# Hash attention and a gated feed-forward on one core: a divisor placed earlier, two pools exchanged, half of the weight sums queued behind the first blocks

## The chip, the cores and the metric

The kernel runs on 1 core of one Trainium2 chip. The metric is the device time of one execution in microseconds (us). A measurement is the median of several executions; a profile is one further execution, with a trace of every engine: TensorE (PE, with its weight loads shown apart as PEld), VectorE (DVE), ScalarE (ACT), GpSimd (POOL) and SyncE (SP), whose work here is to start DMA transfers.

## What is computed

```python
# q, k, v: (4, 8, 768, 64); proj: (64, 6); w_in: (512, 2048); w_out: (2048, 512)
q_bucket = sum(((q @ proj) > 0) * 2**arange(6))      # the same for k_bucket
mask   = q_bucket[..., :, None] == k_bucket[..., None, :]
scores = where(mask, (q @ k.T) / sqrt(64), -1e9)
attn   = softmax(scores) @ v                          # per head
x      = attn.transpose(0, 2, 1, 3).reshape(3072, 512)
h      = x @ w_in
sp     = maximum(h, 0) + log1p(exp(-abs(h)))
out    = (h * erf(sp)) @ w_out                        # (3072, 512)
```

A query attends only to keys in the same hash bucket. The result of the attention, one row per token, goes through two matrix products with a smooth gate between them.

## The kernel before

**Attention.** The 32 heads are taken as 16 pairs. A pair `i` has four groups of scores (`score`, L554): two halves of the queries by two halves of the keys, three key blocks each. ACT takes the exponential of each block (`exponential`, L581), PE weighs the values with it (`weigh`, L639), and DVE adds the exponentials over the key blocks (`sum_keys`, L627, five steps for a pair). `divisor` (L680) lets PE add these sums over the partitions into a PSUM room, `keep_divisor` (L691, ACT) copies it to the tile `z`. The division then goes by small transfers on SP: `spread` (L720) writes `z` to DRAM, `gather` (L727) reads it back as 128x12, `invert` (L737, L740, DVE) takes the reciprocal, `ungather` (L745) and `widen` (L755, two transfers) spread it over the partitions, `normalise` (L766, DVE) multiplies, and `send` (L774) stores the pair's part of x. The last pair, 15, has its own path: its sums go in single steps, and its divisor to `send` are called from the feed-forward, as `late(0)` to `late(2)`.

**Weights.** Beside the attention, 32 pieces of the weights are fetched by POOL (`fetch_weights`, L460) and converted from 64-bit: `square_high` (L474) and `keep_normal` (L481) on ACT, `move_bits` (L488, L496), `mask_bits` (L510, L518) and `add_rest` (L528, L536) on DVE. `square_high` of piece n reuses the buffer that `mask_bits` of piece n-2 reads. `PACE` says after which exponential a piece may be fetched: after number PACE * n / 10 - 2.

**Feed-forward.** x is taken in 6 tiles of 512 tokens and 4 chunks of the hidden size, 24 blocks p. Both products save one of eight multiplications by Strassen's way: a block of the first product has seven products `P1` to `P7` (L1241), which share a few PSUM rooms. `read` (L1259, ACT) takes a room's first result into the tile `h`, `complete` (L1263, DVE) adds the second to it. A later product into the same room waits for that. Then come `lead`, `factor` and `saturate` on ACT (L1271, L1275, L1292), `multiply` and `gate` on DVE (L1281, L1296), sums of h (L1311), and the second product `M1` to `M7` (L1354). The sums that the method needs are made on DVE: of x by `presum_x` (L343) after `load_x` (L331), of w_in by `presum_weights` (L792, eight steps: four in the attention, four as `late(3)` to `late(6)`), of w_out by `presum_w` (L1326), kept by `keep_w` (L1329).

**What sets the order.** `arrange` is a list scheduler that runs when the kernel is built. It gets operations with an engine, an assumed cost, a rank, the operations each comes after, and lateness for signals; it emits them in the order in which they would start. Each engine then works through its own stream in this order, and waits at the first instruction whose semaphores aren't there. The attention (with the weights) is one such plan, the feed-forward with `late(k)` a second. The PE's order in the attention is written out by hand (`order`); the assumed costs move only what the other engines do between.

**Memory.** The attention's pools are closed before the feed-forward's are opened, which take the same memory from the start on. An instruction that first writes a tile of a new pool waits for the last uses of what lay there. The order of the attention's pools is loads of q, k and v (27 KB of a partition), hash bits, exponentials, then `xst` (tiles x, z, r). The feed-forward's: `hp` (h, 8 tiles of 4 KB), `sums`, `wtp` (sums of w_out), `work` (the gate's tiles, 32 KB), `outp`. The last pair keeps its exponentials in the tiles of the loads, which the last steps of `sum_keys` read.

Of the kernel before, what the change touches and what calls it, by code (L numbers as in the profile page):

```python
# [193 lines left out]
def kernel(  # L194
# [12 lines left out]
    B, H, S, D = v.shape  # L207
    NBIT = proj2.shape[1] // 2
    NPAIR = B * H // 2
# [3 lines left out]
    HS = S // 2  # L213
# [203 lines left out]
    def attention():  # L417
        NS = NPAIR * 4
        with (
# [10 lines left out]
            def big(name):  # L430
                return psum.tile([P, 2, 512], F32, name=name, tag="big", bufs=3)
# [9 lines left out]
            pairs = {}  # L441
# [205 lines left out]
            def home(i, what):  # L647

                if i < NPAIR - 1:
                    shape, bufs = {"x": (S, 3), "z": (HS, 1), "r": (S, 2)}[what]  # L650
                    return xst.tile([P, shape], F32, name=what, tag=what, bufs=bufs)
                rows = blocks[1][:, :, :].rearrange("p k t -> p (k t)")
                if what == "x":
                    return x_last, rows[:, 2 * S : 2 * S + HS]
                return rows[:, 0 : HS if what == "z" else S]
# [11 lines left out]
            def divisor(i):  # L667


                d = pairs[i]  # L670
                if i == NPAIR - 1:
                    z = bank("z_ps")[:, 0:HS]
                else:
                    room = pairs[i + 3]["bits"] if i + 3 < NPAIR else big("z_ps")
                    z = room[:, 1, 0:HS]
                d["z_ps"] = z
                for half in range(2):
                    for n in range(4):
                        ab, part = divmod(n, 2)
                        nc.tensor.matmul(  # L680
                            out=z[n * QR : (n + 1) * QR, half * HS // 2 : (half + 1) * HS // 2],
                            lhsT=ones[:, 0:QR],
                            rhs=d["sum"][:, half, ab, part * HS // 2 : (part + 1) * HS // 2],
                            start=True,
                            stop=True,
                        )
# [130 lines left out]
            def op(fn, args, engine, cost, rank, after=(), **more):  # L817
                name = (fn.__name__,) + args
                ops.append(Op(name, engine, cost, rank, lambda: fn(*args), after=after, **more))
# [77 lines left out]

            chain = []
            order = []
            PACE = 19  # L900
            for i in range(NPAIR):
                order += [("score", 4 * i + k) for k in range(4)]
                if i == 0:
                    order.append(("bits", 1))
                if i == NPAIR - 1:
                    order.append(("divisor", i - 1))
                order += [("weigh", 4 * i + k) for k in range(4)]
                if i + 2 < NPAIR:
                    order.append(("bits", i + 2))
                if 0 < i < NPAIR - 1:  # L910
                    order.append(("divisor", i - 1))
            slots = []
            for what, n in order:
                free = slots[-3] if len(slots) >= 3 else ()
                if what == "score":
                    i = n // 4
                    after = (("double_first",) if i == 1 else ("place_bits", i),)
                    for c in range(GC):
                        free = slots[-3] if len(slots) >= 3 else ()
                        pe(score, (n, c), 0.82 if n or c == 2 else 0.17, after + free)  # L920
                        slots.append((("exponential", n, c),))
                elif what == "bits":
                    pe(bits_of, (n,), 0.80 if n > 1 else 1.44, (("start_pair", n),) + free)
                    slots.append((("sign_of", n),) if n > 1 else (("place_first",),))
                elif what == "divisor":
                    if n + 3 < NPAIR:
                        free = ()
                        slots[-1] += (("keep_divisor", n),)
                    else:
                        slots.append((("keep_divisor", n),))  # L930
                    pe(divisor, (n,), 0.72, (("sum_keys", n, last_sum(n)),) + free)
                else:
                    h = n // 2
                    after = (("exponential", n, GC - 1),)
                    if n % 2 == 0:
                        after += (("leave", h - 2), ("leave_plain", (h - 2) // 2))
                    pe(weigh, (n,), 2.0, after)
# [5 lines left out]
            for n in range(NS):  # L943
                for c in range(GC):
                    after = (("score", n, c), ("weigh", n - 4)) + sums_after.get((n - 4, c), ())
# [8 lines left out]
            for i in range(NPAIR):  # L954
                for k, (what, blocks_) in enumerate(sum_steps(i)):
                    after = tuple(("exponential", 4 * i + b // GC, b % GC) for b in blocks_)
                    after += (("sum_keys", i, k - 1), ("sum_keys", i - 1, last_sum(i - 1)))
                    if k == 0:
                        after += (("divisor", i - 2),)
                    if i == NPAIR - 1 and k > 1:  # L960
                        after += (("divisor", i - 1),)
                    wide = what is None or what[2] > 1
                    rank = (3 if i == NPAIR - 1 and k > 2 else 1, 4 * i + 1 + k // 2, k)
                    op(sum_keys, (i, k), "DVE", 1.72 if wide else 0.92, rank, after)
            for i in range(NPAIR - 1):
                op(
                    keep_divisor,
                    (i,),
                    "ACT",
                    0.48,  # L970
                    (0, 4 * i + 6, -1),
                    (("divisor", i), ("spread", i - 1)),
                )
            for h in range(NH):
                i = h // 2
# [3 lines left out]
            for i in range(NPAIR):  # L979
# [52 lines left out]
                    (("ungather", i), ("normalise", i - 2)),  # L1032
                    late=6.5,
                )
                op(normalise, (i,), "DVE", 0.95, (0, n + 8, 4), (("widen", i), ("leave", 2 * i + 1)))
                op(send, (i,), "SP", 0.35, (0, n, 4), (("normalise", i),), late=2.2)
            for n in range(2):
                op(clean, (n,), "POOL", 1.4, (0, 4 * n), (("score", 4 * n + 3, 2),), late=0.3)
            for n in range(len(pieces)):
                op(  # L1040
                    fetch_weights,
                    (n,),
                    "SP" if n < 2 else "POOL",
                    1.0,
                    (0, n),
                    (("start_pair", 1), ("fetch_weights", n - 1), ("add_rest", n - 3), ("exponential", max(PACE * n // 10 - 2, 0), 1)),
                    late=7.0,
                )
                fetched = ("fetch_weights", n)
                op(square_high, (n,), "ACT", 0.68, (1, n, 0), (fetched, ("mask_bits", n - 2)))  # L1050
                op(keep_normal, (n,), "ACT", 0.7, (1, n, 1), (("square_high", n),))
                op(move_bits, (n,), "DVE", 1.05, (2, n, 0), (fetched, ("add_rest", n - 2)))
                op(mask_bits, (n,), "DVE", 1.1, (2, n, 1), (("move_bits", n), ("keep_normal", n)), late=1.5)
                op(add_rest, (n,), "DVE", 1.3, (2, n, 2), (("mask_bits", n),))
            for k in range(4):
                op(
                    presum_weights,
# [136 lines left out]
    def feed_forward(check, late):  # L1194
        again = late is None
        with (
            tc.tile_pool(name="hp", bufs=8) as hp,
            tc.tile_pool(name="sums", bufs=1) as sums,
            tc.tile_pool(name="wtp", bufs=2) as wtp,
            tc.tile_pool(name="work", bufs=1) as work,  # L1200
            tc.tile_pool(name="outp", bufs=1) as outp,
            tc.tile_pool(name="ps_f", bufs=1, space=PSUM) as ps_f,
            tc.tile_pool(name="ps_l", bufs=1, space=PSUM) as ps_l,
# [217 lines left out]
            def op(name, engine, cost, rank, fn, args, **more):  # L1421
                ops.append(Op(name, engine, cost, rank, lambda: fn(*args), **more))
# [132 lines left out]
            def second_ops(p):  # L1555
# [48 lines left out]
                if p < NC4 and not again:  # L1604
                    for k in range(4):
                        op(
                            ("presum_w", p, k),
                            "DVE",
                            0.69,
                            (2, p, k),  # L1610
                            presum_w,
                            (p, k),
                            after=(("presum_w", p, k - 1) if k else ("presum_w", p - 1, 3),),
                            take=("wt", p) if k == 0 else None,
                        )
                    op(
# [83 lines left out]
            if late:  # L1700
# [11 lines left out]
                        late=6.0,  # L1712
                    )
                for k in range(3, 7):
                    op(("late", k), "DVE", 1.2, (2, 1, -7 + k), late, (k,), after=(("late", k - 1),) if k > 3 else ())
                for each in ops:
                    if each.name in (("P5", 2), ("P6", 2), ("P7", 2), ("P3", 2)):
                        each.after += (("late", 6),)
# [107 lines left out]
```

## Time and profile before

| what | value |
|---|---|
| time, 3 runs | 917.02, 918.65, 919.42 us; median 918.65 |
| profiled execution | 916.7 us, its span 914.9 us |
| PE busy | 897.7 us, 98% of the span |
| DVE, ACT busy | 668.7 us (73%), 562.9 us (62%) |
| attention | from the start to about 315.5 us, some 19.17 us a pair |
| feed-forward | from 315.5 us; the last matmul ends at 908.3 us |

The profile gives for every group of instructions its line, engine, output and inputs, the count, the time that it was busy and the mean of one, and the idle time of the engine just before with what ended it ("<-"). The timeline has one row for each run of equal instructions: start, duration, engine, line, and in brackets how long the engine had been idle and who released it. Numbers are us from the start of the span. A matmul of the program shows as two records; a product P of the first kind is 8 records of about 0.216 us, 1.73 us in all.

### The profile page before, as it was taken

To read this page: it belongs to the slowest core of one execution; us is meant where nothing else is said; L and a number is where in the kernel's file an instruction comes from. 1 tells how busy PE (TensorE), PEld (TensorE's weight loads), DVE (VectorE), ACT (ScalarE), POOL (GpSimd) and SP (SyncE) were. 2 spreads that over 40 slices of the span, in tenths; PEclk is the share of its full clock that TensorE was granted. 3 is DMA by queue.
4 is the path that set the end of the run, shared out by engine and by line. 5 is a ranking of instruction groups with operands and counts; after the bars stand their busy time and mean duration, and the time that the engine had idled before them with its cause. 6 is when DMAs were issued, how large, how long until landed. Compare 5 with 4: busy or idle time off the path is not lost.

```text
span 914.9 us, 12791 instructions
## 1 busy us (share of the span) xinstructions
PE 897.7 (98%) x5016; PEld 673.0 (74%) x5016; DVE 668.7 (73%) x837; ACT 562.9 (62%) x808; POOL 58.2 (6%) x95
## 2 busy tenths in 40 slices
PE   9999999999999979999999999999999999999997
PEld 5455544545555558888888888888888888888886
DVE  5999997889989958996566656766676556655652
ACT  7788877778877538854655456555655555545520
POOL 1211211111110000000010001000100000000000
PEclk9999999999999989999999999999999999999999
DMA  9466555567553331021042114211321123101321
GB/s 227 130 166 166 154 175 146 151 189 188 140 171 99 100 122 64 2 80 60 22 104 81 35 47 104 81 35 47 81 104 35 35 58 92 34 31 52 69 69 49
DMA packets 65156, 86.82 MB, mean 95 GB/s; under 512 B 34364, under 2 KB 47772, under 8 KB 65088
## 3 DMA queue, kind: packets, MB, share of 16 engines
q1 hardware_dynamic: 56528, 63.81, 23.6%
q0 software_dynamic: 8112, 21.66, 8.5%
q8 instruction: 41, 0.67, 0.3%
q10 hardware_dynamic: 448, 0.46, 0.2%
q14 instruction: 27, 0.22, 0.1%
HBM read 64.67 MB, written 17.30 MB: 90 GB/s over the span
## 4 chain that ended last, share of the span: by engine, by line
PE 87%; DMA 5%; DVE 5%; ACT 1%; issue 1%; SPq 0%; POOL 0%; DVEq 0%; ACTq 0%; POOLq 0%
PE M L1354 32%; PE X L1241 28%; PE st L554 13%; PE av L639 9%; PE M L1241 2%; DMA r<-rd 2%; DMA rd<-zc 1%; PE bits L838 1%; DMA zd<-z 1%; DVE area L792 1%; DVE area L627 1%; PE bits L680 1%; DMA zc<-zd 1%; DVE x L766 1%; PE warm L800 0%
## 5 line engine op out<-in xcount | busy, mean ns | idle before, releaser
L1281 DVE SCALAR_TENSOR_TENSOR e<-w,e 128x1024 f32<-128x1024 f32 x144 | 173.8, 1220 | 10.3 <-ACT w L1275 5.9
L1241 PE MATMUL X<-area,w_in_sb 128*128 128x256 f32 x680 | 160.7, 379 | 0.0
L1275 ACT ACTIVATE w<-h,cq 128x1024 f32<-128x1024 f32 x144 | 155.5, 1136 | 0.0
L554 PE MATMUL st<-q,k 64*128 64x384 f32 x768 | 155.1, 483 | 0.0
L1263 DVE TENSOR_TENSOR h<-X,h 128x512 f32<-128x512 f32 x65 | 44.8, 689 | 145.0 <-PE X L1241 144.9
L1241 PEld LDWEIGHTS X<-area,w_in_sb 128*128 128x128 f32 x680 | 129.3, 190 | 17.5
L1354 PE MATMUL M<-w_out_sb,h 128*128 128x256 f32 x576 | 141.3, 379 | 0.0
L1241 PE MATMUL X<-area 128*128 128x256 f32 x520 | 123.0, 379 | 0.1
L1354 PEld LDWEIGHTS M<-w_out_sb,h 128*128 128x128 f32 x576 | 109.5, 190 | 14.8
L1259 ACT COPY h<-X 128x512 f32<-128x512 f32 x85 | 49.2, 579 | 110.7 <-PE X L1241 110.7
L1271 ACT ACTIVATE e<-h,cq 128x1024 f32<-128x1024 f32 x48 | 55.0, 1148 | 89.5 <-DVE h L1263 89.5
L1241 PEld LDWEIGHTS X<-area 128*128 128x128 f32 x520 | 98.8, 190 | 13.8 <-DVE h L1263 0.5
L1354 PE MATMUL M<-wt,S 128*128 128x256 f32 x384 | 95.1, 379 | 0.0
L554 PEld LDWEIGHTS st<-q,k 64*128 64x128 f32 x768 | 69.0, 187 | 29.9 <-issue 27.4
L627 DVE TENSOR_TENSOR area<-area 128x1536 f32<-128x1536 f32 (+1 forms) x46 | 79.3, 1724 | 3.4 <-ACT area L581 1.4
L1354 PEld LDWEIGHTS M<-wt,S 128*128 128x128 f32 x384 | 73.0, 190 | 9.9
L581 ACT ACTIVATE e_even<-st 128x768 f32<-128x768 f32 x96 | 70.3, 823 | 0.7 <-PE st L554 0.7
L581 ACT ACTIVATE area<-st 128x768 f32<-128x768 f32 x90 | 67.9, 813 | 0.0
L554 PE MATMUL st<-both 64*128 64x384 bf16 x384 | 63.7, 324 | 2.2 <-ACT z L691 1.7
L639 PE MATMUL av<-e_even,v 128*64 128x385 f32 x384 | 65.6, 490 | 0.0
L1296 DVE TENSOR_TENSOR h<-h,e 128x1024 f32<-128x1024 f32 x48 | 58.0, 1221 | 4.3 <-ACT e L1292 4.3
L639 PE MATMUL av<-area,v 128*64 128x384 f32 x360 | 60.6, 486 | 0.0
(129 smaller groups left out, 981.4 us busy)
## 6 DMA issues: line engine op xcount, KB each, us to landing
wt<-wt SPq DMA_DIRECT2D x24, 768.0 KB, 4.3
raw<-in_w_out_dram POOLq DMA_DIRECT2D x16, 512.0 KB, 4.6
raw<-in_w_in_dram POOLq DMA_DIRECT2D x14, 512.0 KB, 4.8
v<-in_v_dram SPq DMA_DIRECT2D x32, 192.0 KB, 4.7
q<-in_qkT_dram SPq DMA_DIRECT2D x30, 192.0 KB, 3.6
k<-in_qkT_dram SPq DMA_DIRECT2D x30, 192.0 KB, 4.2
r<-rd SPq DMA_DIRECT2D x30, 192.0 KB, 3.5
xs<-x SPq DMA_DIRECT2D x15, 384.0 KB, 2.5
```

The source lines that it names most:

```text
L554: nc.tensor.matmul(out=st[:, ab, 0:HS], lhsT=d["k" + src][rows, keys], rhs=d["q" + src][rows, cols], start=(part == 0), stop=(part == 1),)
L581: nc.scalar.activation(out=e[:, :, 0:HS], in_=st[:, :, 0:HS], func=AF.Exp, scale=scale)
L627: nc.vector.tensor_tensor(out=into, in0=one, in1=two, op=ALU.add)
L639: nc.tensor.matmul(out=d["av", half][rows, 0:w], lhsT=d["v"][:, g * GC + c, rows], rhs=e[:, ab, 0:w], start=(g == 0 and c == 0), stop=(g = ...
L1241: nc.tensor.matmul(out=d[where][:, u, :], lhsT=a[:, kc, f : f + P], rhs=b[:, kc, :], start=(first and u == 0 and kc == 0), stop=(last and ...
L1259: nc.scalar.copy(out=quarter(p, q), in_=st[p][where])
L1263: nc.vector.tensor_tensor(out=h, in0=st[p][where], in1=h, op=ALU.add)
L1271: nc.scalar.activation(out=s, in_=unit(p, v), func=AF.Sigmoid, bias=cq[:, n : n + 1])
L1275: nc.scalar.activation(out=q, in_=unit(p, v), func=AF.Sigmoid, scale=GATE_S[j][0], bias=cq[:, j : j + 1])
L1281: nc.vector.scalar_tensor_tensor(out=s, in0=st[p].pop(("q", v, j)), scalar=GATE_S[j][2], in1=s, op0=ALU.add, op1=ALU.mult,)
L1296: nc.vector.tensor_tensor(out=h, in0=h, in1=st[p].pop(("s", v)), op=ALU.mult)
L1354: nc.tensor.matmul(out=banks[name][:, sub, :], lhsT=a[:, u, sub * P : (sub + 1) * P], rhs=b[:, u, :], start=(c == 0 and k == 0), stop=(c = ...
```

## The change

- `divisor` of pair 14 is issued after the weighing of pair 14, right behind `divisor` of pair 13, and no longer between the scores and the weighing of pair 15. It uses the other half of the PSUM room of pair 13's divisor. `z` gets a second buffer, and `keep_divisor` waits for the spread of two pairs ago in place of one.
- `PACE` is 18 in place of 19, and the assumed cost of `sum_keys`, `normalise` and the conversion's steps on DVE is raised by some per cent. These are inputs to the scheduler.
- In the feed-forward, the pool `work` is opened first, before `hp`.
- `late(3)`, and with it the four steps of `presum_weights` in the feed-forward, and `presum_w` of block 1 get one more thing to come after: `complete` of block 0, quarter 1.

```diff
-                    shape, bufs = {"x": (S, 3), "z": (HS, 1), "r": (S, 2)}[what]
+                    shape, bufs = {"x": (S, 3), "z": (HS, 2), "r": (S, 2)}[what]
...
-                    room = pairs[i + 3]["bits"] if i + 3 < NPAIR else big("z_ps")
-                    z = room[:, 1, 0:HS]
+                    if i == NPAIR - 2:
+                        room = pairs[i - 1]["z_room"]
+                    else:
+                        room = pairs[i + 3]["bits"] if i + 3 < NPAIR else big("z_ps")
+                        d["z_room"] = room
+                    z = room[:, 0 if i == NPAIR - 2 else 1, 0:HS]
...
-            PACE = 19
+            PACE = 18
...
-                if i == NPAIR - 1:
-                    order.append(("divisor", i - 1))
                 order += [("weigh", 4 * i + k) for k in range(4)]
                 if i + 2 < NPAIR:
                     order.append(("bits", i + 2))
                 if 0 < i < NPAIR - 1:
                     order.append(("divisor", i - 1))
+                if i == NPAIR - 2:
+                    order.append(("divisor", i))
...
-                    if n + 3 < NPAIR:
+                    if n != NPAIR - 3:
...
-                    op(sum_keys, (i, k), "DVE", 1.72 if wide else 0.92, rank, after)
+                    op(sum_keys, (i, k), "DVE", 1.76 if wide else 0.93, rank, after)
...
-                    (("divisor", i), ("spread", i - 1)),
+                    (("divisor", i), ("spread", i - 2)),
...
-                op(normalise, (i,), "DVE", 0.95, (0, n + 8, 4), (("widen", i), ("leave", 2 * i + 1)))
+                op(normalise, (i,), "DVE", 1.02, (0, n + 8, 4), (("widen", i), ("leave", 2 * i + 1)))
...
-                op(move_bits, (n,), "DVE", 1.05, (2, n, 0), (fetched, ("add_rest", n - 2)))
-                op(mask_bits, (n,), "DVE", 1.1, (2, n, 1), (("move_bits", n), ("keep_normal", n)), late=1.5)
-                op(add_rest, (n,), "DVE", 1.3, (2, n, 2), (("mask_bits", n),))
+                op(move_bits, (n,), "DVE", 1.14, (2, n, 0), (fetched, ("add_rest", n - 2)))
+                op(mask_bits, (n,), "DVE", 1.15, (2, n, 1), (("move_bits", n), ("keep_normal", n)), late=1.5)
+                op(add_rest, (n,), "DVE", 1.4, (2, n, 2), (("mask_bits", n),))
...
+            tc.tile_pool(name="work", bufs=1) as work,
             tc.tile_pool(name="hp", bufs=8) as hp,
             tc.tile_pool(name="sums", bufs=1) as sums,
             tc.tile_pool(name="wtp", bufs=2) as wtp,
-            tc.tile_pool(name="work", bufs=1) as work,
...
-                            after=(("presum_w", p, k - 1) if k else ("presum_w", p - 1, 3),),
+                            after=(("presum_w", p, k - 1) if k else ("presum_w", p - 1, 3),) + ((("complete", 0, 1),) if p == 1 else ()),
...
-                    op(("late", k), "DVE", 1.2, (2, 1, -7 + k), late, (k,), after=(("late", k - 1),) if k > 3 else ())
+                    op(("late", k), "DVE", 1.2, (2, 1, -7 + k), late, (k,), after=(("late", k - 1) if k > 3 else ("complete", 0, 1),))
```

## The prediction, made before the changed kernel ran

> **What bounds the kernel now.** The page first: PE is busy 897.7 of 914.9 us, so the time is PE's work plus its gaps. Then PE's waits:
>
> ```profile
> PE M L1241 <- DVE h L1263: 5.3, 1, 5.3
> PE M L1241 <- ACT h L1259: 2.1, 1, 2.1
> PE st L554 <- ACT z L691: 1.7, 1, 1.7
> ```
>
> Columns: us in total, times, longest. With the small ones (1.0, 0.3, 0.2) and 6.6 us from the last matmul (908.3) to the end they make 17.2 = 914.9 - 897.7, so nothing else can be won as a gap. Where the two largest lie, the timeline shows:
>
> ```profile
> 319.52 0.96 DVE L627 TENSOR_TENSOR area<-area,v 128x768 f32<-128x768 f32 x1
> 320.71 0.59 ACT L1259 COPY h<-M 128x512 f32<-128x512 f32 x1 [4.59 <-DVE area L627]
> 321.35 3.72 PE L1241 MATMUL M<-area 128*128 128x256 f32 x16 [2.10 <-ACT h L1259]
> 324.10 1.02 DVE L766 SCALAR_TENSOR_TENSOR x<-x,ev,r 128x768 f32<-128x768 f32 x1 [3.61 <-DMA r<-rd]
> 327.56 1.22 DVE L792 TENSOR_TENSOR area<-w_in_sb 128x1024 f32<-128x1024 f32 x1
> 334.03 0.68 DVE L1263 TENSOR_TENSOR h<-M,h 128x512 f32<-128x512 f32 x1
> 334.77 7.99 PE L1241 MATMUL M<-area,w_in_sb 128*128 128x256 f32 x24 [5.26 <-DVE h L1263]
> ```
>
> The first `read` of the feed-forward waits for the last step of `sum_keys`: h lies over tiles that it reads. The second `complete` starts at 334.03, behind `presum_weights` and `presum_w` on DVE; its product had ended by 327.6. A third cost hides in the 24 matmuls after that: 334.77 to 342.60 is 7.83 us where 24 x 0.216 is 5.18. The windows (us, busy by engine, then granted clock, DMA share, GB/s) say why:
>
> ```profile
> 332.20:333.20 1.00, 0.00 (x0) 0.00 (x0) 1.00 (x2) 0.00 (x0) 0.00 (x0) 0.96 0.05 3
> 333.20:334.20 1.00, 0.00 (x0) 0.00 (x0) 0.97 (x3) 0.00 (x0) 0.00 (x0) 0.50 0.00 0
> 338.20:339.20 1.00, 1.00 (x4) 0.73 (x4) 0.00 (x0) 0.58 (x1) 0.00 (x0) 0.50 0.58 197
> 340.20:341.20 1.00, 1.00 (x6) 0.88 (x5) 0.00 (x0) 0.13 (x1) 0.00 (x0) 1.00 0.13 41
> ```
>
> The clock is halved from 333.2 to about 339.8. The stall thus costs 5.26 + 2.65. The gap in the attention:
>
> ```profile
> 201.52 0.67 ACT L474 ACTIVATE keep<-raw 128x512 f32<-128x512 f32 x1 [1.02 <-DVE top L510]
> 202.09 0.56 ACT L847 ACTIVATE sg<-bits,sgn 128x384 bf16<-128x384 f32 x1
> 202.56 0.47 ACT L691 COPY z<-bits 128x384 f32<-128x384 f32 x1
> 203.08 0.34 PE L554 MATMUL st<-both 64*128 64x384 bf16 x2 [1.68 <-ACT z L691]
> ```
>
> A `square_high` that needs DVE stands on ACT ahead of `sign_of` and `keep_divisor`, which free a PSUM room for the scores.
>
> [...] halved 3.8 us after the gap began at 329.4, no loss after the gap of 2.10. [...] Here the small ones take 1.4 to 5.4 us[...].
>
> **The change part by part**, on the time axis of before.
>
> *Pools.* In the changed build's order the first `read` no longer names `sum_keys` but the transfer of `send` of pair 14 (h now lies over x and r), with seven further semaphores behind it. `presum_w` names both sends. So what matters is when that send lands (before: issued at 325.14).
>
> *Divisor 14.* It moves from 306.84 to right behind divisor 13, which takes 296.26 to 297.05. PE's 0.79 and ACT's 0.47 move, nothing is added. It needs the last sum of pair 14, which ended at 296.90, so the wait costs 0 to 0.4; I take 0. On SP, spread and gather of 14 now stand between gather and ungather of 13, and on DVE its invert before the second sum of pair 15. The queues:
>
> ```profile
> 299.27 0.39 SPq L331 DMA_DIRECT2D area<-xs  x1
> 299.75 0.57 SPq L720 DMA_DIRECT2D zd<-z  x1
> 305.19 0.32 SPq L727 DMA_DIRECT2D zc<-zd  x1
> ```
>
> Spread 13 lands behind the 1 MB of `load_x`, so gather 13 stays at 305.19. `presum_x` now stands on DVE before the first sum of pair 15 and waits for that load: estimate 304.8, then 0.65 + 1.7, end 307.15. Spread 14 goes at 305.5, +2.0 (as 283.01 to 285.03) gather 14 at 307.6, +1.6 (as 250.36 to 251.99) 309.2, invert 0.45: DVE is free at 309.65. Then its list up to the end of `normalise` 14, each by the distance of starts in 307.78 to 319.52: two sums 1.67 + 0.93, one `presum_weights` 1.14, three `presum_x` 1.90, ev 0.07, two sums 0.98 + 0.88, `normalise` 13 0.93, sum 0.93, `normalise` 14 1.01, together 10.44: 320.1. The SP chain is just inside: ungather 14 after widen 13 at 310.65, +3.6, +4.2 = 318.5, needed at 319.1. Send at 320.2, +2.7 (median of xs<-x) 322.9; seven met semaphores at about 0.06, 323.4; `read` 0.59. PE resumes at 324.05, against 321.35: **+2.70**, an idle time of 4.8 in place of 2.10. With gathers and spreads of 3.4 each (269.93 to 273.28 is one) it is +5.9; with the SP and DMA steps 1 us better, +1.7.
>
> *Half of the sums later.* Behind the read, DVE has four `presum_w` (322.9 to 325.5), then the first `complete`; the second follows its product directly. PE doesn't wait there: **-5.26**, and the clock's 2.65 with it, if the new gap of 4.8 doesn't halve the clock itself. [...] So **-2.65**, or about 0. The four steps of `presum_weights` now lie at 332.5 to 337.4, where DVE idled for 6.0 (before 342.87). But `judge`'s small DVE steps (1.15) and three `multiply` stand ahead of a `complete` of block 1: DVE from 339 on 1.2 + wait to 340.9 + 1.15 + 2.3 + 0.65 gives 345, PE would ask at 344.3: **+0.8**, 0 to 1.5. After that PE has 14 us of products before it needs the first gate, which is then some 5 us early; the orders after it differ only in a few sums.
>
> *PACE and costs.* 32 pieces in both; each comes up to 1.5 score groups sooner, and none is left for pair 15, where one and its 3.7 us fall away from DVE. DVE needs 8.9 (five sums) + 1.7 + 3.7 x 2.22 = 18.8 of a pair's 19.17, so it may run some 0.9 late for a pair. In ACT's new order I went through all rows where `square_high` stands ahead of `keep_divisor`. The old place at 201.5 is clean. Two new ones are behind a `sign_of`: near 104.5, where DVE was 4 us ahead (cost 0.1), and near 180.7, where `mask_bits` ended at 181.7 in the trace of before: square 0.67 and z 0.47 after it, PE resumes at 183.05 where it wanted 182.1, +1.0. With 0.4 for small ones: 1.5 against 1.9, **-0.4**, from -1.9 to +3.
>
> *Sum.* +2.70 - 5.26 - 2.65 + 0.8 - 0.4 = **-4.8** us. The profiled execution, 916.7, becomes 911.9. It is 1.95 under the median of the runs, 918.65, to which I add the same difference: **913.8**.
>
> **Rivals.**
> - *The clock halves after all* in the gap before the first read. [...] Against: the gap of before was 5.26[...]. It hides the 0.8: -4.8 + 1.9 = -2.9, **915.7**.
> - *ACT's order costs more*: the places near 104.5, 120, 180.7 and 200 each stall PE by 1 us or so, since DVE has no slack left. For: 18.8 of 19.17, and waits for r and zc of up to 2.2. Against: DVE was early in the first pairs. -4.8 + 3.4 = -1.4, **917.2**.
> - *The send becomes the bound, slower.* Gather and spread of pair 14 take what spread 13 takes, 5.4, and 3.4; DVE stands behind invert, everything to the send lands 5.2 later, at 328.1. The gap of 10 surely halves the clock. -2.9 + 5.2 = +2.3, **920.9**. It decides from a landing at 325.8 on.
> - *All goes well*: the send lands at 321.9, no wait at judge, no stall at 180.7: -4.8 - 1.0 - 0.8 - 1.2 = -7.8, **910.9**.
> - *The change does nothing*: excluded, the built orders differ at each of these places.
>
> **How the numbers follow.** This kernel's runs spread by 0.26%, so about 0.3% (2.8 us) can be told from no change. Chances: forecast 0.43, halved clock 0.22, ACT's order 0.13, slower 0.12, all well 0.10. The forecast and all well lie under 915.9, and half of the halved clock's spread of 1 us or more: 0.64 faster. The rest of that, ACT's order, and a little of the slow case fall within 0.3%: 0.25; slower 0.11. The range takes in all well with its bound of 1 us and most of the slow side: 909.5 to 919.0.
>
> **What would show it.** In the profile after: PE's waits name `read` with 4 to 5.5 us and no `complete` with 5; the send of pair 14 lands near 323; the last z of the attention stands near 298; no halved clock around 333; a wait for z of about 1 us near 182 and none near 203. I am wrong if `read` waits past 326, if the attention's waits exceed 3 us, or if PE has a gap past 345 that I don't have.

## The result, and the profile after

| | before | after |
|---|---|---|
| time, median | 918.25 us (917.02 to 919.42, 4 runs) | 909.79 us (907.90 to 910.26, 4 runs) |
| profiled execution | 916.7 us, span 914.9 us | 910.26 us, span 908.2 us |
| PE busy | 897.7 us | 897.4 us |
| first product of the feed-forward | 315.53 us | 313.43 us |
| first matmul of the second product | 364.20 us | 358.23 us |

The changed kernel takes 0.9904 of the time before, with a 95% interval of 0.9884 to 0.9924. It is 8.5 us faster; 4.8 us were forecast, and the time lies just inside the range. PE is busy for as long as before; its gaps have changed. PE's three longest waits in the profile after (us in total, times, longest):

```profile
PE M L1245 <- ACT h L1263: 2.9, 1, 2.9
PE warm L804 <- DVE ones L250: 1.0, 1, 1.0
PE M L1245 <- DVE h L1267: 0.7, 1, 0.7
```

Lines from L676 on have moved by 4. The wait for a second `complete` (5.3) has become one of 0.7 at another place, and the attention's wait for `z` isn't there. The timeline where the feed-forward begins:

```profile
315.49 1.01 DVE L770 SCALAR_TENSOR_TENSOR x<-x,ev,r 128x768 f32<-128x768 f32 x1
...
318.84 0.69 DVE L1330 TENSOR_TENSOR wt<-w_out_sb 128x512 f32<-128x512 f32 x1 [0.48 <-DMA xs<-x]
319.45 0.59 ACT L1263 COPY h<-M 128x512 f32<-128x512 f32 x1 [5.43 <-DMA xs<-x]
320.09 6.63 PE L1245 MATMUL M<-area 128*128 128x256 f32 x16 [2.94 <-ACT h L1263]
...
329.54 0.69 DVE L1267 TENSOR_TENSOR h<-M,h 128x512 f32<-128x512 f32 x1 [7.48 <-PE M L1245]
331.00 5.34 PE L1245 MATMUL M<-area,w_in_sb 128*128 128x256 f32 x24
```

`normalise` of pair 14 runs at 315.49, 2.06 us after the first product; before it ran at 324.10, 8.57 after it. The transfer of its send has landed by 318.84, where `presum_w` on DVE was waiting for it; `read` follows at 319.45, PE after an idle time of 2.94. The second `complete` is on time, and DVE idles ahead of it. But the 16 matmuls at 320.09 take 6.63 us, where the same 16 took 3.72 before. The windows (us, busy by engine, then granted clock, DMA share, GB/s):

```profile
318.20:319.20 1.00, 0.00 (x0) 0.00 (x0) 0.52 (x2) 0.00 (x0) 0.00 (x0) 0.99 0.14 52
319.20:320.20 1.00, 0.11 (x1) 0.11 (x1) 0.97 (x3) 0.59 (x1) 0.00 (x0) 0.50 0.00 0
325.20:326.20 1.00, 1.00 (x4) 0.80 (x4) 0.00 (x0) 0.00 (x0) 0.00 (x0) 0.59 0.00 0
```

The clock is halved in this execution too, from 319.2 to 326.0, 2.0 us after PE went idle at 317.15. The place in the attention that the prediction feared:

```profile
177.56 0.69 DVE L510 SCALAR_TENSOR_TENSOR top<-top,keep 128x512 int32<-128x512 int32 x1
...
181.30 0.66 ACT L474 ACTIVATE keep<-raw 128x512 f32<-128x512 f32 x1
...
181.86 0.48 ACT L695 COPY z<-bits 128x384 f32<-128x384 f32 x1
```

A `square_high` does stand ahead of `z`, but the step of `mask_bits` that reads its buffer (`keep`, L510) had ended at 178.25, 3.0 us before it: PE doesn't wait.

### The profile page after: what moved, and what is told of

It reads as the page before. It is cut to its first block, busy times and chain, and to the rows that moved or that the text cites. A ratio compares the mean times of both kernels' runs of the same rounds, so it can differ in the third digit from the quotient of the medians.

```text
span 908.2 us, 12781 instructions
## 1 busy us (share of the span) xinstructions
PE 897.4 (99%) x5016; PEld 673.2 (74%) x5016; DVE 669.5 (74%) x837; ACT 563.3 (62%) x808; POOL 58.3 (6%) x95
## 4 chain that ended last, share of the span: by engine, by line
PE 96%; DVE 2%; DMA 1%; issue 0%; ACT 0%; SPq 0%; ACTq 0%; DVEq 0%
PE M L1358 32%; PE X L1245 29%; PE st L554 16%; PE av L639 13%; PE M L1245 3%; PE bits L842 1%; PE bits L684 1%; DMA zd<-z 1%; PE warm L804 0%; DVE area L627 0%; PE bits L374 0%; DMA xs<-x 0%; PE z_ps L684 0%; DMA zc<-zd 0%; DVE x L770 0%
```

## The experiments

They were run in four groups, each beside runs of the kernel before on its own chip; "ratio" is against those, with its 95% interval. Gaps of PE in us are from the one profiled execution of each: the waits for `z` in the attention, the one at the first `read`, and those for a `complete` (0.66 or 0.7 is the one behind `judge`, in block 1). "Halved" is for how many us of this execution the clock was halved, up to the last matmul. Times of different groups are compared by ratio. The groups are: the four kernels after with one part put back; after once more, the later sums alone, the gap filled and h placed early; the other three parts alone and h placed early with the weight sums put back; the last two rows.

| kernel | median, us | ratio to before | z | read | complete | halved |
|---|---|---|---|---|---|---|
| before | 918.25 | 1 | 1.7 | 2.10 | 5.26 | 6.8 |
| after | 909.79 | 0.9904 (0.9884 to 0.9924) | 0 | 2.94 | 0.66 | 6.8 |
| after, once more | 910.27 | 0.9908 (0.9887 to 0.9929) | 0 | 2.94 | 0.66 | 3.4 |
| after, pools put back | 907.53 | 0.9922 (0.9903 to 0.9941) | 0 | 2.04 | 0.66 | 0 |
| after, weight sums put back | 909.41 | 0.9938 (0.9919 to 0.9956) | 0 | 3.40 | 0.33 | 0 |
| after, divisor put back | 915.27 | 0.9993 (0.9984 to 1.0003) | 0 | 7.36 | 0.7 | 6.8 |
| after, PACE and costs put back | 912.92 | 0.9973 (0.9958 to 0.9987) | 1.5 | 3.91 | 0.66 | 3.4 |
| before, later sums alone | 912.34 | 0.9931 (0.9909 to 0.9954) | 2.1 | 2.18 | 0.66 | 3.4 |
| before, sooner divisor alone | 914.39 | 0.9964 (0.9953 to 0.9975) | 2.8 | 3.41 | 0 | 3.4 + 3.4 |
| before, PACE and costs alone | 913.67 | 0.9966 (0.9953 to 0.9978) | 0 | 0 | 5.33 | 6.8 |
| before, pools alone | 919.62 | 1.0019 (1.0008 to 1.0029) | 3.8 | 9.03 | 0 | 3.4 + 10.2 |
| after, gap filled on PE | 908.84 | 0.9904 (0.9886 to 0.9922) | 0 | 0.28 | 0.66 | 0 |
| after, h placed early | 905.71 | 0.9867 (0.9847 to 0.9886) | 0 | 0 | 0.66 | 0 |
| the same, weight sums put back | 910.46 | 0.9926 (0.9908 to 0.9943) | 0.2 | 0 | 2.94 | 3.4 |
| after, only the costs put back | 914.64 | 0.9967 (0.9952 to 0.9982) | 2.9 | 3.0 | 0.7 | 3.4 + 3.4 |
| after, only PACE put back | 916.61 | 0.9981 (0.9961 to 1.0001) | 6.6 | 3.5 | 0.7 | 10.2 + 3.4 |

### Each part put back, from the kernel after

The pools:

```diff
-            tc.tile_pool(name="work", bufs=1) as work,
             tc.tile_pool(name="hp", bufs=8) as hp,
             tc.tile_pool(name="sums", bufs=1) as sums,
             tc.tile_pool(name="wtp", bufs=2) as wtp,
+            tc.tile_pool(name="work", bufs=1) as work,
```

> The kernel after, with only the order of the feed-forward's pools put back (hp first, work fourth). Theory: each wait is where the trace of after shows it, and the pools set only what the first read waits for: no longer the transfer of the send of pair 14 (319.45 in after), but the last step of sum_keys (ends at 318.36). PE's first gap shrinks from 2.94 to about 2.1 us, the rest stays: about 908.9 us, or 907 to 908 where the shorter gap halves the clock for a shorter time. Then this part of the change costs some 0.9 us by itself. Rival: the pools are what keeps something else from waiting (the sums of w_out, the gate's first tiles): a new wait appears and it is slower than after, 911 or more.

The gap at the read shrinks to 2.04 us, as the theory has it, and its profile shows no halved clock. The ratio can't be told from that of after, so the 0.9 us stand on the profile alone. No new wait of PE of more than 0.2 us appears in its profile.

The weight sums:

```diff
-after=(("presum_w", p, k - 1) if k else ("presum_w", p - 1, 3),) + ((("complete", 0, 1),) if p == 1 else ()),
+after=(("presum_w", p, k - 1) if k else ("presum_w", p - 1, 3),),
...
-after=(("late", k - 1) if k > 3 else ("complete", 0, 1),))
+after=(("late", k - 1),) if k > 3 else ())
```

> The kernel after, with only the queue of the weight sums put back (late(3) and presum_w of block 1 free to stand ahead of the second complete). Theory of the prediction: the later sums are what took the stall of 5.26 us and its halved clock (2.65) away, so both come back, 909.8 + 5.3 + 2.6 = 917.7 us. Rival: the stall before was made by DVE being late behind normalise of pair 14, which the sooner divisor has moved from 324.10 to 315.49. DVE's list from 318.84 is then 4 x 0.66 + 4 x 1.22 + 0.68 + 2 x 0.66 = 9.5 us, so the second complete starts at 328.3; its product ends at about 329.3 in after with its halved clock, so there is no stall (909.8 us), or one of about 2 us where the clock isn't halved, 909.5 to 912 us in all.

The stall doesn't come back. PE's waits in its profile:

```profile
PE M L1245 <- ACT h L1263: 3.4, 1, 3.4
...
PE M L1245 <- DVE h L1267: 0.3, 1, 0.3
```

The second `complete` started at 328.19, where the rival's sum gave 328.3, and PE waited 0.33 us for it, without a halved clock. In this profile the later sums are worth next to nothing once the divisor is sooner; the prediction gave them the whole 5.26. The ratio alone doesn't show that: 0.9938 is some 3 us above that of after, in intervals that barely overlap. But beside the kernel with the pools put back, of the same group, it is 1.9 us slower by the medians, and the waits of the two profiles account for 1.7 of that (3.40 and 0.33 against 2.04).

The divisor of pair 14, with one buffer of `z` (the diff of the change backwards, its first, second, fourth and fifth piece and the line with `spread`):

> The kernel after, with only the divisor of pair 14 put back between the scores and the weighing of pair 15 (with one buffer of z and keep_divisor behind the spread of the pair before). Theory: with the pools of after the first read then waits for a send of pair 14 that follows normalise 14 at about 322 to 323; it lands at about 326, the gap grows from 2.94 to about 10 us and halves the clock as now: 909.8 + 7 = about 917 us. So the pools and the divisor belong together. Rival: the send isn't what the read waits for by much, and the gap is some 4 to 5 us: 911 to 912 us. For the attention: if its wait for z near 203 is back (1.7 us), it was the divisor's part of the change (second z, later spread) that removed it; if not, PACE and the costs.

The theory holds in kind: the `read` waits for the send, which was issued at 321.02 and had landed by 323.32. The gap is 7.36 us, in place of the 10 expected, with a halved clock behind it, and all but nothing of the gain is left. The attention has no wait for `z`, so it isn't the second `z` that emptied it.

PACE and the costs (19, and the old numbers):

> The kernel after, with PACE 19 and the old assumed costs. Theory: PACE and the costs are what emptied the attention of waits; ACT's order there is again that of before but for the end, so the wait for z near 203 comes back (1.9 us), and one piece of the weights with its 3.7 us on DVE stands in pair 15 again, so that normalise 14 and its send come up to 3.7 us later: 909.8 + 1.9 + 0 to 3.7 = 911.7 to 915.4 us. Rival: the second z buffer and the later spread emptied the attention, and PACE is worth nothing there: 909.8 to 910.5 us.

The median is within the theory's range: a wait for `z` of 1.5 us is back, and the gap at the read is 3.91 in place of 2.94.

### Each part alone, on the kernel before

The later sums alone:

> The kernel before, with the later weight sums alone (late(3) and presum_w of block 1 behind complete of block 0, quarter 1). Theory from the runs so far: the stall of 5.26 us comes from two things together, a late normalise of pair 14 (to 325.12) and the weight sums between it and the second complete; either part of the change removes it alone. Then DVE goes from 325.12 through four sums of w_out (2.6) and the first complete (0.7) to the second at 328.4, in time for the product at 329.4: no stall, 5.3 us won and its halved clock, the gap of 2.10 and the attention's 1.9 stay: some 6 to 8 us below before. Rival: only the sooner divisor removes it, and the time is that of before less 0 to 2 us.

No stall: `normalise` 14 ran at 326.11, the first and second `complete` in one go at 329.58, and PE went on at 331.17 without a wait. The ratio, 0.9931, is 6.3 us (4.2 to 8.4). So here the sums are worth what the prediction gave them. The profile has one thing more, a halved clock in the attention, from 185.43 to 188.85, after a wait of only 2.11 us:

```profile
184.19 0.34 PE L554 MATMUL st<-both 64*128 64x384 bf16 x2 [2.11 <-ACT z L691]
```

The sooner divisor alone:

> The kernel before, with the sooner divisor of pair 14 alone (second z, keep_divisor behind the spread two pairs ago). Theory: it removes most of the stall at the second complete by itself, since DVE no longer stands at normalise 14 until 325.12: with the last sum at 320.9 as in the kernel with PACE put back, its list of 9.5 us ends at 330.4 and PE asks at about 329.5, a stall of 1.6 us in place of 5.26 and mostly no halved clock; the gap at the read is 2 to 2.6 us and the attention's wait for z stays: some 4 to 6 us below before. Rival: without the later sums the stall stays at 5 us: the time of before.

The stall of 5.26 goes here as well, in this kernel without the later sums:

```profile
PE M L1245 <- ACT h L1263: 3.4, 1, 3.4
PE st L554 <- ACT z L695: 2.8, 1, 2.8
```

```profile
318.50 3.72 PE L1245 MATMUL M<-area,w_in_sb 128*128 128x256 f32 x16
...
331.76 1.99 PE L1245 MATMUL M<-area,w_in_sb 128*128 128x256 f32 x8
...
333.86 0.69 DVE L1267 TENSOR_TENSOR h<-M,h 128x512 f32<-128x512 f32 x1
```

But only half of that is the divisor's. The second `complete` starts 15.36 us after the first product, where it was 18.50 before: 3.1 sooner. And PE comes to the fifth product 13.26 us after the first, where it was 10.26 (315.53 to 325.79): 3.0 later, for the gap at the read is 3.41 in place of 2.10, with a halved clock behind it. The ratio is 3.3 us, less than expected, as that gap, a wait for `z` of 2.8 and two halved clocks (the other one behind that wait) stand against it.

PACE and the costs alone:

> The kernel before, with PACE 18 and the new costs alone. Theory: it takes away the attention's wait for z near 203 (1.9 us) and shifts all that follows by as much; the stall at the second complete stays at about 5 us, as it hangs on the transfers behind the divisor, and so does its halved clock; the gap at the read is 2.1 us or up to 1 us less, as DVE has one piece less in pair 15: 2 to 3 us below before. Rival: the piece that pair 15 no longer has moves normalise 14 and the stall too: 4 us or more below before.

```profile
PE M L1241 <- DVE h L1263: 5.3, 1, 5.3
```

The stall stays to the tenth, as the theory said; the wait for `z` is gone, and so is all of the 2.10 at the read (up to 1 was expected): without the last piece of the weights DVE ends the last `sum_keys` at 317.0, 3.0 us after the first product, where it was 5.0 before. By the ratio 3.1 us, by the medians 4.1.

The pools alone:

> The kernel before, with the other order of the feed-forward's pools alone. Theory: the first read waits for the send of pair 14, whose normalise ends at 325.12; with 2.7 us to landing and 0.6 for the waits the read goes at 328.4, PE's first gap is 9.8 us, and the stall at the second complete shrinks to 0 to 1.9 us since PE comes there later: 9.8 to 11.7 us of gaps in place of 7.4, 2.4 to 4.3 us slower than before. Rival: the send isn't late enough to matter behind the last sum, the time is that of before.

```profile
PE M L1241 <- ACT h L1259: 9.0, 1, 9.0
PE st L554 <- ACT z L691: 3.8, 2, 2.9
```

Slower by 0.19%, 1.7 us, where 2.4 to 4.3 were expected: the send was issued at 328.57 and had landed by 330.88, PE waits 9.03 us at the read for it, and the stall at the second `complete` is hidden behind that. By itself this part of the change loses.

### The clock, and a better place for h

The kernel after once more, unchanged, and one whose gap PE fills with work on nothing. The latter's edit, ahead of the third product:

```diff
+                st["calls"] = st.get("calls", 0) + 1
+                if st["calls"] == 3 and not again:
+                    fill = bank("fill")
+                    for n in range(12):
+                        nc.tensor.matmul(out=fill[0:D, 0:P], lhsT=ones, rhs=ones[:, 0:1].broadcast_to([P, P]), start=True, stop=True)
```

> The kernel after, unchanged, on the same chip as the next three, to compare with them; and a look at whether another execution halves the clock in the same place. Theory: [...] some executions halve it after the gap of some 3 us and others don't, and the times spread by the 2.9 us that it costs: 906 to 910 us. Rival: it is halved in each execution, and the spread is something else.

> The kernel after, with 12 matmuls of 128 columns on ones, into a PSUM bank that nothing else uses at that time, queued on PE just ahead of the product that waits for the first read; they fill some 2.6 of its gap of 2.9 us. Theory: [...] the clock is never halved here, and 2.9 us are won in those executions where after has it: its mean falls by 1 to 2.9 us and its spread is smaller. Rival: the halved clock has another cause than PE's idling (the DMA traffic or the load of the other engines at that time): it is still there, and the time is that of after.

The second profile of after has the same gap of 2.94 us, and the clock is halved for 3.4 us rather than 6.8. In the ten timed runs of after the mean clock is 0.995 to 0.998, and 0.998 in the three fastest, 907.84 to 908.74. With the gap filled the clock isn't halved in the profile. First the row of the fill, then two windows:

```profile
317.71 2.88 PE L1226 MATMUL fill<-ones 128*64 128x128 f32 x24
```

```profile
318.20:319.20 1.00, 1.00 (x11) 1.00 (x10) 0.93 (x1) 0.00 (x0) 0.00 (x0) 1.00 0.91 356
320.20:321.20 1.00, 0.72 (x6) 0.45 (x5) 0.97 (x3) 0.59 (x1) 0.00 (x0) 1.00 0.00 0
```

PE idles 0.28 us at this place in place of 2.94, and all its six runs have a mean clock of 0.998 or 0.999, so the rival falls: here the halved clock goes with PE's idling. The ratio, 0.9904 against 0.9908 of the same group, doesn't show the gain; the medians differ by 1.4 us, which is inside the intervals.

Then h where nothing late lies: in the attention `xst` is opened first, in the feed-forward `hp` last.

```diff
+            tc.tile_pool(name="xst", bufs=1) as xst,
             tc.tile_pool(name="load", bufs=3) as load,
             tc.tile_pool(name="bitp", bufs=1) as bitp,
             tc.tile_pool(name="ep", bufs=1) as ep,
-            tc.tile_pool(name="xst", bufs=1) as xst,
...
-            tc.tile_pool(name="work", bufs=1) as work,
-            tc.tile_pool(name="hp", bufs=8) as hp,
             tc.tile_pool(name="sums", bufs=1) as sums,
-            tc.tile_pool(name="wtp", bufs=2) as wtp,
             tc.tile_pool(name="outp", bufs=1) as outp,
+            tc.tile_pool(name="wtp", bufs=2) as wtp,
+            tc.tile_pool(name="work", bufs=1) as work,
+            tc.tile_pool(name="hp", bufs=8) as hp,
```

> The kernel after, with its pools in another order: in the attention x, z and r (xst) first; in the feed-forward h last, so that h lies over the exponentials and the buffers of the weights' conversion, whose last reader is a step of sum_keys that ends at about 307.8. The first read then waits for nothing but its product. Theory: the gap of 2.94 goes, with it the halved clock, and nothing stands behind it, since the second product into that room has its read done by then and the first complete, at about 321.0 behind four sums of w_out, isn't needed before the second block: -2.9 and up to -2.9, 904 to 906 us beside 907 to 910 of after. Rival: the wait was covering another, the complete of quarter 3 or the divisor of pair 15 behind the last step of sum_keys: PE waits 1 to 3 us a little later, and 1 us or less is won.

```profile
PE warm L804 <- DVE ones L250: 1.0, 1, 1.0
PE M L1245 <- DVE h L1267: 0.7, 1, 0.7
```

The gap is gone and no other took its place. This is the fastest of all: 0.9867 of before, and 4.6 us below after by the medians of the same group. The same with the weight sums put back:

> The kernel with h placed early (c_h_early), with the queue of the weight sums put back to that of before. Theory: in the kernel after the later sums were worth only some 0.3 us because PE's wait at the first read (3.4 us with the sums put back) gave DVE the time to get through the list ahead of the second complete. Without that wait DVE needs, from 318.36, 4 x 0.66 + 4 x 1.2 + 0.68 + 2 x 0.66 = 9.4 us, the second complete ends at 328.5, and PE asks for it at about 324.9: a stall of some 3.6 us, in some executions with a halved clock: 905.7 + 3.6 + 0 to 2.9 = 909 to 912 us. Rival: the later sums are worth little anywhere: 906 us.

```profile
PE M L1245 <- DVE h L1267: 2.9, 1, 2.9
```

A stall of 2.94 us at the second `complete`, with a halved clock. So the later sums, worth 0.3 us in the profile with the sums put back into the kernel after, are worth some 5 once nothing holds PE back at the read (ratios 0.9926 and 0.9867).

### PACE or the costs

> The kernel after, with the old assumed costs, but PACE 18. Theory: a piece that is fetched sooner is also converted sooner on DVE, so mask_bits is done before the square_high that waits for it, whatever the exact order on ACT; and none is left for pair 15. PACE is all of it: no wait for z in the attention, a gap of about 2.9 us at the read, 908 to 910 us. Rival: the costs hold the order in which ACT's z comes ahead of a square_high: a wait for z of 1 to 2 us is back, 911 us.

> The kernel after, with PACE 19, but the new assumed costs. Theory (PACE is all of it): a wait for z of 1 to 2 us in the attention, and a gap of about 3.9 us at the read, as in the run with both put back: 912 to 913.5 us. Rival: the costs do it: no wait for z, 909 to 911 us.

The theory falls. PACE 18 with the old costs has a wait for `z` of 2.9 us, PACE 19 with the new costs one of 6.6; neither can be told from the kernel with both put back (0.9973). Either one alone gives an order on ACT in which a `square_high` waits for DVE ahead of `z`. In the last kernel:

```profile
199.55 0.17 DVE L741 TENSOR_SCALAR zc<-zc 128x12 f32<-128x12 f32 x1 [4.99 <-DMA zc<-zd]
199.91 5.35 DVE L627 TENSOR_TENSOR area<-area 128x1536 f32<-128x1536 f32 x3
206.42 0.69 DVE L510 SCALAR_TENSOR_TENSOR top<-top,keep 128x512 int32<-128x512 int32 x1
207.15 0.67 ACT L474 ACTIVATE keep<-raw 128x512 f32<-128x512 f32 x1 [6.34 <-DVE top L510]
207.72 0.46 ACT L695 COPY z<-bits 128x384 f32<-128x384 f32 x1
208.23 0.51 PE L554 MATMUL st<-both 64*128 64x384 bf16 x2 [6.59 <-ACT z L695]
```

`invert` stood 4.99 us on DVE for a `gather`; three sums and the mask came that much later, `square_high` waited for the mask, `z` for ACT, PE for `z`. What such a place costs depends on when a small transfer lands. That is argued, not tried; it fits the spread of these two kernels' runs (910.07 to 918.98, and 911.56 to 920.12) and the different waits for `z` in the kernels that share before's PACE and costs, 1.5 to 3.8 us. In the nine profiles of kernels with PACE 18 and the new costs, PE has no wait for `z` in eight and one of 0.2 us in the ninth; in the seven others it has 1.5 to 6.6.

## Why the prediction was right in direction and short in size

The terms of the sum, forecast and as the two profiled executions have them:

| term | forecast | profiles |
|---|---|---|
| gap at the first read | +2.70 | +0.84 |
| second `complete` | -5.26 | -5.26 |
| halved clock | -2.65 | +0.26 |
| behind judge | +0.8 | +0.66 |
| attention | -0.4 | -2.1 |
| last stores land sooner | none | -0.7 |
| sum | -4.8 | -6.3 |

The profiled executions differ by 6.4 us, their spans by 6.7, so some 0.4 us of the spans are in no term. The medians differ by 8.46: the profile of before was 1.5 us below its median, that of after 0.5 above. Four steps failed.

- **"To which I add the same difference."** Of the 4.0 us between the forecast 913.8 and 909.79, 1.6 lie between the profiled execution that was forecast, 911.9, and 910.26. The other 2.4 are this term: the prediction put the median of after 1.95 above its profile, because it was so before, and gave no reason. It was 0.5 below. The profile of after is the slowest of its four runs, with the lowest mean clock (0.995; the others 0.996 to 0.998), so the halved clock is likely a part of it. Why the profile of before was faster than the four runs beside it stays open.
- **The attention's term, -0.4.** It counted a new wait of about 1.0 us near 180.7, from the end of a `mask_bits`, 181.7, in the trace of before. But PACE 18 also moves the pieces on DVE. The `square_high` that stands there after is the 22nd and waits for a step of the 20th `mask_bits`, which ended at 178.25 (181.7 is the end of this step of the 19th). The order on ACT was read rightly there, the time of its partner was not moved along. The attention lost its old waits (1.7 for `z`, 0.2 for an exponential) and got none: -2.1. That PACE and the costs do this, and only together, is shown by the runs with one put back.
- **"Gather 13 stays at 305.19", and "DVE is free at 309.65".** Set on the axis of before (+2.10), `gather` 13 went at 303.48, the load of x had landed by 303.4 (estimated 304.8) and the second `invert` ended at 308.27, 1.4 us early. From there the working held: DVE's list to the end of `normalise` 14 took 10.33 us (forecast 10.44), the send 2.3 (2.7), the semaphores and other waits ahead of `read` 0.6 (0.5). So the idle time was 2.94 in place of 4.8, and the term +0.84 in place of +2.70.
- **"So -2.65, or about 0."** That a gap of 4.8 us mostly spares the clock was the author's estimate: the trace of before had a halved clock behind a gap of 5.26 us, none behind one of 2.10, and no gap between. In the profile after the clock was halved behind 2.94, and the term is +0.26 in place of -2.65. The rival of a halved clock came true in it, though not its time, since the other terms were better. (In before the clock fell 3.6 us after PE had gone idle at 329.51; the 3.8 of the prediction is misread, but no term rests on it.)

The largest term was right in size but ascribed to one part. The stall at the second `complete` needed two things: DVE held by `normalise` 14 until 325.12, and 8.3 us of weight sums between that and the second `complete` (ten steps, four of which stay there after the change). The later sums alone remove it. The sooner divisor alone takes 3.1 us from it, and the longer gap at the read hides the rest. Putting the sums back into the kernel after returns 0.33 us of it, and 2.94 where no gap at the read is left. So the parts don't add, as these waits show. The ratios alone don't show it: singly they give -6.3, -3.3, -3.1 and +1.7 us, together -11.0, and the change gives -8.4 to -8.8, but each has an interval of 1 to 2 us to either side. The new order of the pools loses: 1.7 us alone on before, 0.9 at the read in the profile of after. An order of pools won here where `h` got memory that is free early, as in the fastest kernel.

The rival "the send becomes the bound" is what the kernel with the divisor put back shows; in the change itself the send landed at 318.84, which is 320.94 on the axis of before, 4.9 us short of the 325.8 from which that rival decides.

## What to carry to other kernels

Before ascribing a stall to one cause, ask what else would have to be late for it to occur: here two queues met, one repair sufficed alone, the other only together with a longer wait elsewhere, and in the changed kernel the later sums paid only after the first wait of the next stage was gone. A wait that hides another has to be counted too. When an edit moves a producer, move its time in the working too, not only its place in the order. One profiled execution isn't the median: say why the two should differ by as much after as before, or widen the range. Open the pools of the next stage so that the tile that it writes first lies over what the last stage finished first.

## What the runs showed of the hardware that was not expected

In these profiles the length of PE's gap alone doesn't tell whether the clock is halved. The shortest gap with a halved clock behind it is the 2.11 us in the attention of the kernel with the later sums alone. In the same profile the gap of 2.18 at the read has none (the granted clock is 1.00 from 320.0 to 332.0), and neither has the gap of 3.40 with the weight sums put back (1.00 from 316.0 to 335.0), while that of 3.41 with the sooner divisor alone has one.

Nor is the time from the last matmul to the fall the same in them. After gaps of 2.94 us in both profiles of after, the clock fell 2.03 us after the last matmul in the first and 2.97 in the second; with the divisor put back it was 5.28 (PE idle from 317.16, clock halved from 322.44).

The sixteen halved stretches up to the last matmul, in twelve of the sixteen profiles, last about 3.4, 6.8 or 10.2 us. That of the second profile of after is 3.42 us (320.82 to 324.24), that of the first 6.84 (319.18 to 326.02). In the first PE was busy from 320.09 on and had the halved clock for 5.93 us more. What sets the fall and the return was not shown.

Nor was it shown how often the gap of after halves the clock; both of its profiles have it. Of the ten timed runs of after, seven have a mean clock below 0.998. That is a rough sign only, as the mean counts the idle end of a run as well (in the first profile the clock is halved again from about 906.3 to the end at 908.2, behind the last matmul): of the five runs with h placed early, whose profile has no such gap, two have 0.997.
